# A decay product two units ahead, scatters in one unit, and layer 2 ordered by kind

## The chip, the cores and the metric

The kernel runs on one core of a Trainium2 chip. The core has five engines that run their own instruction streams and wait for each other by semaphores: TensorE (PE in the profile; its weight loads are listed as PEld), VectorE (DVE), ScalarE (ACT), GpSimd (POOL) and SyncE (SP), which mostly issues transfers. The metric is the device time of one execution in microseconds, as the median of several runs.

## The reference

The program computes three things in a row. First a decaying linear attention over 4 batches, 8 heads, 768 positions and a head size of 64: in blocks, `out = (q k^T * D) v + (q * lam^(i+1)) S`, with a state `S = lam^block * S + (k * lam^(block-1-i))^T v`. The result is 3072 rows of 512 numbers. Then a first mixture of experts over these rows:

```python
logits = x @ w_gate + modality_bias[modality_id]
e_idx = np.argmax(logits, axis=1)
gate_w = softmax(logits)[row, e_idx]
for e in range(8):
    mask = e_idx == e
    h = np.maximum(x[mask] @ w1[e], 0.0)          # 512 -> 1024
    out[mask] = gate_w[mask, None] * (h @ w2[e])  # 1024 -> 512
```

Then a second mixture of the same shape with other weights, without a bias, for those rows only for which `x @ w_skip > 0`; its result is added to the row, and the other rows pass through.

## The kernel before

**Precision.** Large products are made from two float32r parts of each operand, a high and a low one: high times high, low times high and high times low. A raw weight `raw1` or `raw2` is split by ScalarE into the high part (`w1h`, `w2h`, a rounding copy) and by VectorE into the low part (`w1l`, `w2l`, the raw value less the high one). A float32 product of the attention runs as two passes, each with its own weight load.

**Attention.** The work is cut into N = 24 units `(c, b)`: six chunks of 128 positions times four batches, chunk by chunk. Instructions stand in an order written out by hand in the loop over `i` (`tc.manual_schedule()`), and each engine runs its own in that order. For a unit, `stage_s` makes the scores and VectorE multiplies them by the decay mask `dm` into `P`; `stage_t` transposes k and VectorE scales it into `kd`; `stage_q` (GpSimd) makes `qs`, q times the decay table `ltab`, and `t0`, the old state times the block decay; `stage_inter` multiplies `qs` by the state; `stage_av` multiplies `P` by v and ScalarE copies the sum to `xts`; `stage_kv` makes the state's update, which VectorE adds to `t0` into `sc_` and ScalarE copies into `sd`; `stage_x` transposes the output to rows and SyncE stores them in `xs1`. Units of the first chunk have no state and no `qs`, those of the last chunk no `t0`. k and q are loaded four units ahead. Before the first unit `spin` keeps TensorE at work with products of a constant, and the table `ltab` is built by VectorE from a tile `lead`.

**Routing.** After each chunk the four units' logits are made (`route_1`, `route_2`), the expert is chosen (`route_3`, a chain of small VectorE instructions that ends in the one-hot `oh` and the running counts `rs`), ranks and gates follow (`route_4`), and `route_5` scatters an index row for each of four row groups from GpSimd's queue into the table `tab[0]`. The list `sc` holds the scatters that are still to come. In unit 17 the counts so far choose the expert with the most rows; its weights and its first 256 rows are fetched while the attention still runs (`load_ix`, `gather_x`, `ld_w1_half`, `ld_w2`). `behind` makes a weight load wait for the gathered rows.

**The layers.** Each mixture works through slots of 256 rows of one expert, as two blocks j of 128. `trans_x` transposes the gathered rows into `xth` and `xtl`; `layer1` makes 8 column groups f of 128 with 12 products each, and after every second f ScalarE (`hh`) and VectorE (`hl`) take the result from one of three banks; `layer2` makes for a block 8 chunks c with 3 products each, and ends with a scaled result `x2r`. `steps[f]` are functions that run after group f and its evacuation, `mids[f]` those between its products and its evacuation, `hooks[n]` those after chunk n. `first1` and `first2` write out the first slot of each layer, in which the last routing step, the slot table (`table`, a chain of VectorE instructions in three parts, each started by `next(tb)`), the index reads, the gathers and the weight splits of what follows all have to be done. Later slots run in `slots`.

Of the kernel before, what the change touches and what calls it, by code (L numbers as in the profile page):

```python
# [9 lines left out]
F32 = mybir.dt.float32  # L10
# [8 lines left out]
P = 128  # L19
# [16 lines left out]
def body(ctx: ExitStack, tc: tile.TileContext, qkv, cpk, w1, w2, wgr, out, dbg=None):  # L36
# [284 lines left out]
    def low_w2(c, eng=nc.vector):  # L321
        eng.tensor_tensor(out=w2l[c], in0=raw2[:, 2 * c:2 * c + 2], in1=f32(w2h[c]), op=ALU.subtract)  # L322
# [97 lines left out]
    with ExitStack() as actx:  # L420
# [45 lines left out]
        def spin(n):  # L466
            for _ in range(n):
                nc.tensor.matmul(banks[6][:, 0:P], keepm, keepm, start=True, stop=True)

        lead = wk.tile([P, NP, P], F32, tag="qs", name="lead")  # L470
# [72 lines left out]
        def stage_q(i):  # L543
            c, b = units[i]
            if c == 0:
                return
            qs = wk.tile([P, NP, P], F32, tag="qs", name="qs")
            nc.gpsimd.tensor_tensor(out=qs, in0=loaded[i][1], in1=ltab, op=ALU.mult)
            qss[i] = qs
            if c < NC - 1:  # L550
                t0 = wk.tile([P, NP, C], F32, tag="t0", name="t0", bufs=1)
                nc.gpsimd.tensor_tensor(out=t0, in0=sc_[b], in1=bc(ltab[:, :, P - 1:P], [P, NP, C]), op=ALU.mult)
                t0s[i] = t0
# [42 lines left out]
        spin(8)  # L596
        stage_s(0)
        stage_t(0)
        spin(2)
        for i in range(N):  # L600
            rc = i // B - 1 if i >= B and i % B == 0 else None
            rd = i // B - 1 if i >= B and i % B == 1 else None
            if i + 1 < N and i + 1 not in qss:
                stage_q(i + 1)
# [32 lines left out]
            if i == N - 3:  # L637
                stage_q(N - 1)
                got0 = gather_x(0, 0, 4 * B * P)
# [9 lines left out]
            for _ in range(2 if i in (17, 18, 21, 22) else 1):  # L649
                if sc:  # L650
                    route_5(*sc.pop(0))
# [156 lines left out]
    def layer2(which, kk, j, hooks={}, cs=range(8)):  # L808
# [10 lines left out]
        if 7 not in cs:  # L819
            return  # L820
# [20 lines left out]
    def first1():  # L841
        tb = table(0)

        def last_x():
            high(1, (2, 3))
            low(1, (2, 3))
            stage_x(NC * B - 1, ptr[0])
            route_1()
            high_w2(0)
            low_w2(0, nc.gpsimd)  # L850

        def mid():
            route_2(NC - 1)
            route_3(NC - 1)

# [27 lines left out]
    def first2():  # L883
# [3 lines left out]
        layer1(0, {0: la, 3: lambda: rb(pcnt[1]), 4: lambda: next(tb), 5: lambda: split_w2([1]),  # L887
               6: lambda: split_w2([2]), 7: lambda: split_w2([3])}, mids={1: rk}, lead=True)
# [11 lines left out]
        layer2(1, 0, 0)  # L900
        next(tb)
        fl = flag(1, 1)
        layer2(1, 0, 1, {5: lambda: trans_x(1, 1, ptr), 6: lambda: split_next(1, 1, fl)})

# [178 lines left out]
```

## Time and profile before

| | before |
|---|---|
| median of 3 runs | 682.98 us (682.23 to 684.29) |
| the profiled execution's own time | 682.28 us |
| its span, first to last instruction | 680.4 us |
| TensorE busy | 659.4 us (97%), 5408 products |
| weight loads busy | 588.4 us (86%) |
| VectorE busy | 435.5 us (64%) |
| ScalarE busy | 261.5 us (38%) |
| GpSimd busy | 225.0 us (33%) |
| mean granted TensorE clock | 0.994 |

The profile is of one execution, and all times in it count from its first instruction. The time of that execution is 1.9 us longer than its span. A busy TensorE is not one at its peak: products are pipelined, and their ends are modelled. L764 and the like are lines of the kernel before. A row's bracket gives the idle time before it and what ended it.

### The profile page before, as it was taken

What the parts mean: (1) busy time and instruction counts of PE and PEld (TensorE: products, weight loads), DVE (VectorE), ACT (ScalarE), POOL (GpSimd) and SP (SyncE); (2) the same over time, 40 slices, a digit from 0 to 9 for tenths busy, and PEclk for the clock granted to TensorE, in tenths of its full rate; (3) what the DMA queues carried; (4) which work ended last, traced back from release to release, by engine and by line L of the source; (5) the groups of instructions that cost most, each with busy time, mean ns of one, the idle gap of its engine ahead of it and who ended that gap; (6) DMA issues with size and microseconds to landing.
All of it is one profiled execution on the core that took longest, in us unless ns stands there. A gap on an engine that the chain in (4) does not pass through costs nothing. (4 is left out here: it accounts for less than half of the span.)

```text
span 680.4 us, 16335 instructions
## 1 busy us (share of the span) xinstructions
PE 659.4 (97%) x5408; PEld 588.4 (86%) x5408; DVE 435.5 (64%) x1147; ACT 261.5 (38%) x461; POOL 225.0 (33%) x284
## 2 busy tenths in 40 slices
PE   9999999999999999999999999998999999999993
PEld 8899987888988898889889988897999899988892
DVE  7655678764887716869778227967236575759650
ACT  5444435422212225822122227441224644566520
POOL 4265656443242231243422333323211112203321
PEclk9999999999999999999999999999999999999997
DMA  8978777459331133893211211724616557657500
GB/s 261 301 217 217 227 206 247 156 172 373 126 118 52 50 127 119 289 302 131 86 50 31 94 66 37 257 92 116 240 63 241 180 176 276 218 188 263 190 4 30
DMA packets 60797, 112.08 MB, mean 165 GB/s; under 512 B 18816, under 2 KB 18944, under 8 KB 60528
## 3 DMA queue, kind: packets, MB, share of 16 engines
q1 hardware_dynamic: 48688, 89.07, 39.6%
q0 software_dynamic: 9744, 20.47, 9.0%
q8 instruction: 63, 1.03, 0.7%
q10 hardware_dynamic: 2224, 0.86, 0.5%
q14 instruction: 78, 0.64, 0.3%
HBM read 86.44 MB, written 30.06 MB: 171 GB/s over the span
## 5 line engine op out<-in xcount | busy, mean ns | idle before, releaser
L764 PE MATMUL bank<-xth,w1h 128*128 128x256 f32 x672 | 188.3, 281 | 1.1 <-DVE hl L774 0.8
L764 PE MATMUL bank<-xtl,w1h 128*128 128x256 f32 x672 | 185.8, 278 | 1.7 <-issue 1.6
L764 PE MATMUL bank<-xth,w1l 128*128 128x256 f32 x672 | 186.7, 278 | 0.0
L814 PE MATMUL bank<-w2h,hh 128*128 128x512 f32 x360 | 144.7, 402 | 0.0
L815 PE MATMUL bank<-w2l,hh 128*128 128x512 f32 x360 | 140.9, 392 | 1.1 <-DVE w2l L322 1.1
L816 PE MATMUL bank<-w2h,hl 128*128 128x512 f32 x360 | 141.3, 393 | 0.3 <-DVE hl L796 0.3
L764 PEld LDWEIGHTS bank<-xth,w1h 128*128 128x128 f32 x672 | 126.4, 188 | 3.5 <-issue 1.1
L764 PEld LDWEIGHTS bank<-xth,w1l 128*128 128x128 f32 x672 | 126.6, 188 | 2.1 <-DVE hl L774 1.7
L764 PEld LDWEIGHTS bank<-xtl,w1h 128*128 128x128 f32 x672 | 126.0, 188 | 1.4 <-DVEq L836 0.7
L771 ACT ACTIVATE hh<-bank 128x512 fp32r<-128x512 f32 x84 | 50.3, 598 | 182.7 <-PE bank L764 172.1
L161 POOL DMA_INDIRECT out_dram<-x2r,it x43 | 52.5, 1220 | 192.6 <-DVE x2r L829 105.6
L774 DVE SCALAR_TENSOR_TENSOR hl<-bank,hh 128x512 fp32r<-128x512 f32 (+1 forms) x100 | 58.4, 601 | 84.7 <-ACT hh L771 84.3
L717 DVE CUSTOM_DVE_ANT_0 xtl<-x2r,wgb 128x512 fp32r<-128x512 f32 x108 | 74.3, 692 | 14.4 <-issue 9.1
L816 PEld LDWEIGHTS bank<-w2h,hl 128*128 128x128 f32 x360 | 67.6, 188 | 16.0 <-DVE hl L796 0.7
L815 PEld LDWEIGHTS bank<-w2l,hh 128*128 128x128 f32 x360 | 67.7, 188 | 15.7 <-DVE w2l L322 2.5
L161 POOL DMA_INDIRECT tab<-pk,rows x28 | 33.3, 1190 | 141.0 <-issue 85.8
L814 PEld LDWEIGHTS bank<-w2h,hh 128*128 128x128 f32 x360 | 67.7, 188 | 12.8
L165 POOL DMA_INDIRECT xg<-xs,it x54 | 58.2, 1078 | 26.4 <-issue 13.7
L322 DVE TENSOR_TENSOR w2l<-raw,w2h 128x1024 fp32r<-128x1024 f32 x47 | 54.7, 1219 | 4.7 <-ACT w2h L319 2.8
L826 ACT ACTIVATE x2r<-bank,it 128x512 f32<-128x512 f32 x26 | 17.9, 689 | 100.3 <-PE bank L816 89.4
L319 ACT CAST w2h<-raw 128x1024 fp32r<-128x1024 f32 x48 | 49.1, 1051 | 18.8 <-issue 12.0
L316 DVE TENSOR_TENSOR w1l<-raw,w1h 128x512 fp32r<-128x512 f32 x88 | 53.9, 685 | 0.5 <-ACT w1h L315 0.3
(211 smaller groups left out, 835.5 us busy)
## 6 DMA issues: line engine op xcount, KB each, us to landing
raw<-in_w_dram SPq DMA_DIRECT2D x96, 512.0 KB, 6.3
kq<-in_qkv_dram SPq DMA_DIRECT2D x48, 256.0 KB, 4.2
xs<-x2r SPq DMA_DIRECT2D x28, 256.0 KB, 2.1
v<-in_qkv_dram SPq DMA_DIRECT2D x24, 256.0 KB, 3.9
xs<-xr SPq DMA_DIRECT2D x24, 256.0 KB, 6.2
xs<-xgm SPq DMA_DIRECT2D x7, 512.0 KB, 4.8
wgb<-in_wgr_dram SPq DMA_DIRECT2D x1, 2304.0 KB, 13.6
xg<-xs,it POOLq DMA_INDIRECT x54, 4.1
```

What stands on the lines that cost most here:

```text
L161: nc.gpsimd.indirect_dma_start(out=dst, out_offset=bass.IndirectOffsetOnAxis(ap=idx, axis=0), in_=rows, in_offset=None, bounds_check=dst.s ...
L165: return nc.gpsimd.indirect_dma_start(out=rows, out_offset=None, in_=src, in_offset=bass.IndirectOffsetOnAxis(ap=idx, axis=0), bounds_chec ...
L316: nc.vector.tensor_tensor(out=w1l[c][:, s], in0=raw1[:, c, s], in1=f32(w1h[c][:, s]), op=ALU.subtract)
L319: nc.scalar.copy(out=w2h[c], in_=raw2[:, 2 * c:2 * c + 2])
L322: eng.tensor_tensor(out=w2l[c], in0=raw2[:, 2 * c:2 * c + 2], in1=f32(w2h[c]), op=ALU.subtract)
L717: nc.vector.tensor_tensor_reduce(out=xtl[kk % 2][:, :, j * P:(j + 1) * P], in0=x2r[kk % 2][j].rearrange("p (c t) -> p c t", t=P), in1=wgb[ ...
L764: nc.tensor.matmul(o, w[c][:, fs], x[:, c, :], start=(n == 0), stop=(n == 11))
L771: nc.scalar.activation(out=a, in_=pt, func=AF.Relu)
L774: nc.vector.scalar_tensor_tensor(out=b[:, q_], in0=pt[:, q_], scalar=0.0, in1=f32(a[:, q_]), op0=ALU.max, op1=ALU.subtract)
L814: nc.tensor.matmul(p2[j], a, w2h[g][:, i], start=(n == 0), stop=False)
L815: nc.tensor.matmul(p2[j], a, w2l[g][:, i], start=False, stop=False)
L816: nc.tensor.matmul(p2[j], b, w2h[g][:, i], start=False, stop=(n == 7))
```

## The change

- `spin` makes products of 64 columns instead of 128, 15 and 1 of them instead of 8 and 2.
- `stage_q` makes only `qs` and runs two units ahead instead of one, with three buffers instead of two (the tile `lead` has one of them); `t0` moves into a new function `stage_d`, one unit ahead as before, with two buffers instead of one. The separate call of `stage_q` for the last unit goes.
- In unit 17 four scatters are issued, in unit 18 none; before it was two and two.
- The first low part `w2l` of the first layer is made by VectorE after `route_3`, and not by GpSimd.
- In `first2` ranks and gates (`rb`) come ahead of the evacuation of group 3; the high parts of w2 stay in the steps 5 to 7, the low ones come after layer 1; the table's third part comes before layer 2; and layer 2 runs over both blocks by kind, first all products of `hh` with `w2h`, then of `hl` with `w2h`, then of `hh` with `w2l`. The transposes for slot 1 stand after 39 of the 48 products, before after 42.
- The end of `layer2` becomes a function `finish`.

```diff
@@ -318,8 +318,8 @@
     def high_w2(c):
         nc.scalar.copy(out=w2h[c], in_=raw2[:, 2 * c:2 * c + 2])
 
-    def low_w2(c, eng=nc.vector):
-        eng.tensor_tensor(out=w2l[c], in0=raw2[:, 2 * c:2 * c + 2], in1=f32(w2h[c]), op=ALU.subtract)
+    def low_w2(c):
+        nc.vector.tensor_tensor(out=w2l[c], in0=raw2[:, 2 * c:2 * c + 2], in1=f32(w2h[c]), op=ALU.subtract)
 
     def split_w2(cs=range(4)):
         for c in cs:
@@ -465,9 +465,9 @@
 
         def spin(n):
             for _ in range(n):
-                nc.tensor.matmul(banks[6][:, 0:P], keepm, keepm, start=True, stop=True)
-
-        lead = wk.tile([P, NP, P], F32, tag="qs", name="lead")
+                nc.tensor.matmul(banks[6][:, 0:C], keepm, keepm[:, 0:C], start=True, stop=True)
+
+        lead = wk.tile([P, NP, P], F32, tag="qs", name="lead", bufs=3)
         nc.vector.memset(lead, 0.0)
 
         def ladder(r, lm, first, acts=False):
@@ -544,11 +544,14 @@
             c, b = units[i]
             if c == 0:
                 return
-            qs = wk.tile([P, NP, P], F32, tag="qs", name="qs")
+            qs = wk.tile([P, NP, P], F32, tag="qs", name="qs", bufs=3)
             nc.gpsimd.tensor_tensor(out=qs, in0=loaded[i][1], in1=ltab, op=ALU.mult)
             qss[i] = qs
-            if c < NC - 1:
-                t0 = wk.tile([P, NP, C], F32, tag="t0", name="t0", bufs=1)
+
+        def stage_d(i):
+            c, b = units[i]
+            if 0 < c < NC - 1:
+                t0 = wk.tile([P, NP, C], F32, tag="t0", name="t0")
                 nc.gpsimd.tensor_tensor(out=t0, in0=sc_[b], in1=bc(ltab[:, :, P - 1:P], [P, NP, C]), op=ALU.mult)
                 t0s[i] = t0
 
@@ -593,15 +596,17 @@
             return [nc.sync.dma_start(out=raw1[:, c:c + 2, n * D:n * D + D], in_=src[:, c:c + 2, n * D:n * D + D]) for c in (0, 2)][0]
 
         sc = []
-        spin(8)
+        spin(15)
         stage_s(0)
         stage_t(0)
-        spin(2)
+        spin(1)
         for i in range(N):
             rc = i // B - 1 if i >= B and i % B == 0 else None
             rd = i // B - 1 if i >= B and i % B == 1 else None
-            if i + 1 < N and i + 1 not in qss:
-                stage_q(i + 1)
+            if i + 2 < N:
+                stage_q(i + 2)
+            if i + 1 < N:
+                stage_d(i + 1)
             if rc is not None:
                 route_1()
             if i == 20:
@@ -635,7 +640,6 @@
             if 0 < i < N - 1:
                 stage_s(i + 1)
             if i == N - 3:
-                stage_q(N - 1)
                 got0 = gather_x(0, 0, 4 * B * P)
             if i < N - 1:
                 stage_x(i, psX)
@@ -646,7 +650,7 @@
                 sc += [(rd, t) for t in range(B)]
             if i + 1 < N:
                 stage_t(i + 1)
-            for _ in range(2 if i in (17, 18, 21, 22) else 1):
+            for _ in range(4 if i == 17 else 2 if i in (21, 22) else 1):
                 if sc:
                     route_5(*sc.pop(0))
             if 2 <= i < 4:
@@ -816,8 +820,25 @@
             nc.tensor.matmul(p2[j], b, w2h[g][:, i], start=False, stop=(n == 7))
             if n in hooks:
                 hooks[n]()
-        if 7 not in cs:
-            return
+        if 7 in cs:
+            finish(which, kk, j)
+
+    def layer2_wide(which, hooks):
+        n = 0
+        for kind in range(3):
+            for j in range(2):
+                js = slice(j * P, (j + 1) * P)
+                for c in range(8):
+                    x = (hh, hl, hh)[kind][c // 4][:, c % 4, js]
+                    w = (w2h, w2h, w2l)[kind][c // 2][:, c % 2]
+                    nc.tensor.matmul(p2[j], x, w, start=(kind == 0 and c == 0), stop=(kind == 2 and c == 7))
+                    if n in hooks:
+                        hooks[n]()
+                    n += 1
+                if kind == 2:
+                    finish(which, 0, j)
+
+    def finish(which, kk, j):
         g = XG(which, kk)[j]
         ix = IT(which, kk)[:, j]
         gate = ix[:, 1:2].bitcast(F32)
@@ -847,11 +868,11 @@
             stage_x(NC * B - 1, ptr[0])
             route_1()
             high_w2(0)
-            low_w2(0, nc.gpsimd)
 
         def mid():
             route_2(NC - 1)
             route_3(NC - 1)
+            low_w2(0)
 
         def late():
             route_4(NC - 1)
@@ -884,8 +905,10 @@
         la, rk, rb = router(itl)[1:4]
 
         tb = table(1)
-        layer1(0, {0: la, 3: lambda: rb(pcnt[1]), 4: lambda: next(tb), 5: lambda: split_w2([1]),
-               6: lambda: split_w2([2]), 7: lambda: split_w2([3])}, mids={1: rk}, lead=True)
+        layer1(0, {0: la, 4: lambda: next(tb), 5: lambda: high_w2(1), 6: lambda: high_w2(2), 7: lambda: high_w2(3)},
+               mids={1: rk, 3: lambda: rb(pcnt[1])}, lead=True)
+        for c in range(1, 4):
+            low_w2(c)
         for i in range(1, 4):
             load_ix(1, i)
         got = gather_x(1, 1)
@@ -897,11 +920,9 @@
                               reason="the rows first")
         ld_w2(e)
         gather_x(1, 2)
-        layer2(1, 0, 0)
         next(tb)
         fl = flag(1, 1)
-        layer2(1, 0, 1, {5: lambda: trans_x(1, 1, ptr), 6: lambda: split_next(1, 1, fl)})
-
+        layer2_wide(1, {38: lambda: trans_x(1, 1, ptr), 41: lambda: split_next(1, 1, fl)})
         return fl, is_full(ei[1][0:1, 3 * KT + 1:3 * KT + 2])
 
     def slots(which):
```

## Rows read from the trace of the kernel before

**Rows 1.** TensorE's waits over the whole run: us in total, times, longest.
```profile
PE bank L366 <- DMA xg<-xs,it: 2.1, 3, 1.0
...
PE pmi L137 <- DVE oh L125: 0.8, 1, 0.8
```
**Rows 2.** Two stretches by engine: busy us (instructions), granted clock, DMA.
```profile
0.00:8.00 8.00, 6.74 (x40) 6.19 (x40) 4.59 (x9) 5.04 (x11) 5.48 (x43) 1.00 0.75 237
465.00:469.00 4.00, 4.00 (x19) 3.28 (x18) 3.72 (x17) 0.00 (x0) 1.91 (x3) 1.00 0.33 80
```
**Rows 3.** Timeline of the start: start, us, engine, line, instructions.
```profile
1.26 3.49 PEld L468 LDWEIGHTS bank<-keepm 128*128 128x128 f32 x16 [1.26 <-DVE keepm L464]
...
4.97 2.08 PE L522 MATMUL bank<-kq 64*128 64x128 f32 x16
...
7.08 1.42 DVE L529 TENSOR_TENSOR P<-bank,dm 128x256 f32<-128x256 f32 x4
...
7.37 0.53 PEld L468 LDWEIGHTS bank<-keepm 128*128 128x128 f32 x4
```
**Rows 4.** Timeline of units 17 to 19.
```profile
95.81 0.98 POOL L161 DMA_INDIRECT tab<-pk,row  x1 [0.30 <-issue]
96.27 1.85 DVE L206 TENSOR_TENSOR eid<-t_p,t_g 128x8 f32<-128x8 f32 x1
...
96.81 1.28 POOL L548 TENSOR_TENSOR qs<-kq,ltab 128x512 f32<-128x512 f32 x1
...
97.13 0.60 PE L537 MATMUL bank<-ident,kq 128*128 128x128 f32 x4
...
98.14 1.16 PE L561 MATMUL bank<-qs,sd 128*128 128x128 f32 x8 [0.42 <-POOL qs L548]
...
100.04 0.98 PE L569 MATMUL bank<-P,v 128*64 128x128 f32 x13 [0.16 <-DVE P L529]
```
**Rows 5.** Timeline from the last early scatter to the gathered rows.
```profile
100.96 0.97 POOL L161 DMA_INDIRECT tab<-pk,row  x1 [0.30 <-issue]
...
106.96 0.40 SPq L351 DMA_DIRECT2D it<-tab  x1
...
110.78 1.07 POOL L165 DMA_INDIRECT xg<-xs,it  x1 [0.15 <-issue]
...
115.77 1.06 PE L561 MATMUL bank<-qs,sd 128*128 128x128 f32 x8
...
119.23 1.09 PE L569 MATMUL bank<-P,v 128*64 128x128 f32 x16
```
**Rows 6.** Transfers issued from 95 to 120 us: median us to landing.
```profile
xg<-xs,it POOLq DMA_INDIRECT x2, 6.6
```
**Rows 7.** Timelines at units 16 and 23: one instruction, alone and beside GpSimd's.
```profile
89.97 0.19 DVE L122 SCALAR_TENSOR_TENSOR sc<-d,pri 128x32 f32<-128x32 f32 x1
...
125.74 2.39 POOL L322 TENSOR_TENSOR w2l<-raw,w2h 128x1024 fp32r<-128x1024 f32 x1 [4.21 <-ACT w2h L319]
125.75 2.43 DVE L122 SCALAR_TENSOR_TENSOR sc<-d,pri 128x32 f32<-128x32 f32 x1
```
**Rows 8.** Timelines of the second layer's first slot, four engines.
```profile
453.70 0.69 DVE L774 SCALAR_TENSOR_TENSOR hl<-bank,hh 128x512 fp32r<-128x512 f32 x1 [1.35 <-ACT hh L771]
...
459.19 1.04 ACT L319 CAST w2h<-raw 128x1024 fp32r<-128x1024 f32 x1
...
460.07 2.35 DVE L322 TENSOR_TENSOR w2l<-raw,w2h 128x1024 fp32r<-128x1024 f32 x2
...
461.33 0.50 PE L815 MATMUL bank<-w2l,hh 128*128 128x512 f32 x1 [1.07 <-DVE w2l L322]
...
463.66 1.41 POOL L165 DMA_INDIRECT xg<-xs,it  x1 [4.93 <-DMA it<-tab]
466.86 1.08 POOL L165 DMA_INDIRECT xg<-xs,it  x1 [1.79 <-issue]
...
471.17 0.66 PE L366 MATMUL bank<-ident,xg 128*128 128x128 f32 x4 [0.98 <-DMA xg<-xs,it]
```

## The prediction

> **What bounds the kernel now.** I read the list of TensorE's waits first, then the stretches around each wait as a timeline of all engines, and last the landing times of the transfers. TensorE sets the end: of a 680.4 us span it is busy for 659.4, and the products follow each other. A change can therefore only win back the few places where TensorE stands still. The list of waits has the larger of them [rows 1]: 2.1 us for gathered rows (three times, two of them in the attention's last unit, one in layer 2 of the second layer) and 0.8 for the routing's `oh`. The timelines add 1.07 for a low part of w2 [rows 8], one late `qs` [rows 4], and the time before the first unit, in which products run at half pace [rows 3]. The change touches each of these places. All costs below are shifts of TensorE's next product.
>
> **The spin at the start.** Sixteen loads, one for each of the two passes of eight products, occupy 3.49 us, 0.218 apart [rows 3]. In a later stretch four such loads take 0.53, about 0.11 apart [rows 3]. So the first stretch runs at 1.2 GHz and the later one at 2.4, though the view of stages gives a granted clock of 1.00 for all of 0 to 8 us [rows 2] and the pace alone tells. The step is near 7.0 us, where the products of the first unit change pace; before it TensorE had run since 1.26. The edit makes 15 products of 64 columns out of 8 of 128, which is 30 loads instead of 16, each still of 128 columns by 128 rows. No row shows such a load under so short a product. Bounds: if a pass costs its columns, it halves to 0.109 and the spin takes 3.3 us. If the load sets the pace, it stays at 0.218. I take the load, because the loads fill their stretch without a gap: nothing shows that one takes less than its 0.218. Then 26 of the 30 passes fit between 1.26 and 7.0, four more at 0.11 end at 7.45, and the scores of unit 0 begin near 7.5 instead of 4.97. They then run at full pace, about 1.1 us where they took 2.08, and VectorE can take them up 1.2 us after their start, at 8.7 instead of 7.08 [rows 3]: **+1.6 us**. From there on TensorE and VectorE hand over to each other without a gap, so the delay stays. At the lower bound the scores begin 0.2 us sooner, but VectorE takes up `P` at 7.08 without idle time before it [rows 3], so it is busy until then: 0. Cutting the second spin from 4 passes of 128 to 2 of 64 columns gives nothing: TensorE waits there for the mask product `P`.
>
> The rule of the Trainium skill on this stands in its page "TensorE: Matmul & The Clock Gate", section "LDWEIGHTS (loading the stationary operand)": the time of a load goes with the stationary operand's columns, and the product's own length does not enter. Its figure for 128 columns, 107 ns, agrees with the 0.11 of the later stretch; by it as an estimate 30 loads at half pace would take 6.4 us, against 3.3 if columns counted.
>
> **`qs` two units ahead, four scatters in one unit.** In unit 17 GpSimd does two scatters and only then `qs` for unit 19 (96.81 to 98.09). VectorE's `eid`, eight columns wide, lasts 1.85 us, from 96.27 to 98.12, until that `qs` product has run [rows 4]; an instruction four times as wide takes 0.19 [rows 7]. TensorE's transposes end at 97.57 (four from 97.13, 0.109 each), and its next batch starts at 98.14. The products on `P`, whose mask VectorE could make only after `eid`, go on at 100.04 [rows 4]. After the edit `qs` for 19 is finished a unit earlier, and only scatters stand in GpSimd's queue then. `eid` falls to 0.19, `P` is done 1.66 us sooner, by 98.4, and the products on it can go on at 97.57 + 1.0 (eight products) + 0.1 = 98.7: **-1.3 us**. What is queued behind the four scatters: at a pitch of 0.98 + 0.30 (the one at 95.81 [rows 4]) they leave at 94.5, 95.8, 97.1 and 98.4 and end at 99.4; then come `qs` for 20, 1.28 like its neighbour, to 100.7, and the decay product for unit 19 to 101.4. The batch that needs that `qs` comes a whole unit, about 5 us, after the one of 98.14. VectorE wants the decay product near 100.4 and gets it 1 us late; the state it feeds is used four units on, and the next `P`, which waits behind it on VectorE, is wanted only after TensorE's transposes and its batch on `qs`, some 2 us. Without that cover it would cost up to 1.0. In the other units no wait for `qs` is there to be won.
>
> **The first gather.** Index rows for slot 0 are read by SyncE only when the fourth scatter of this group has landed: it leaves at 100.96, the read at 106.96, the gather at 110.78, and its rows take 6.6 us [rows 5, 6]. TensorE ends its batch of 115.77 at 116.66, does eight transposes (0.87) and starts the next at 119.23 [rows 5]: 1.6 us lost, of which 1.5 is wait. With the last scatter leaving 2.5 us sooner the read leaves near 104.4 and the gather near 107.2 (GpSimd's last `qs` is done by 105.5, since it no longer waits for a buffer). The rows land by 113.8 and 115, before TensorE asks for them at 115.3 and 115.8: **-1.5 us**. Bounds: 0 if the scatters land as late as now, since the first half of w1 is on the queues then; 1.6 if all is hidden. The w2 load, which SyncE holds back behind this gather, starts about 3 us sooner, which no wait asks for.
>
> **First w2l on VectorE.** GpSimd's subtraction lasts 2.39 us from 125.74. VectorE's `sc`, 32 columns, starts at 125.75 and lasts 2.43, where the same instruction takes 0.19 a few units earlier [rows 7]. `oh` follows it, and TensorE's counting product waits for that [rows 1]. Without the subtraction on GpSimd `sc` is 2.24 us sooner, and the wait goes. But VectorE now does the subtraction itself, at 1.2 us (two take 2.35 [rows 8]), so all that stands behind it on VectorE (the high-low split, row numbers, the scatters, the slot table, the other low parts) comes only 2.24 - 1.2 = 1.0 us sooner. TensorE runs into the low parts in layer 2, where the last ones are just in time today. I take **-1.1 us**; bounds -0.5 and -1.5.
>
> The Trainium skill has the cause: "SBUF — State Buffer", section "SBUF: two separate sides", says that a VectorE instruction with two SBUF inputs and a GpSimd instruction that reads SBUF contend for one port pair, which is an exclusive lock for a whole instruction. The 2.43 beside the 2.39 agrees with it.
>
> **The second layer's first slot.** TensorE waits 1.07 us for the second low part of w2, until 461.33, and 0.98 for gathered rows of slot 1, until 471.17 [rows 8]. A product of this layer takes 0.23 (4.00 us hold 18 loads, one of them cut by the edge [rows 2]). Layer 2 starts at 461.33 - 1.07 - 8 x 0.23 = 458.5 or so. Ordered by kind, the low parts are needed after 32 products, at 466, and VectorE has them near 463.8, since nothing but the order of its work changes: that wait goes. A new one comes in: the high part of the fourth chunk (459.19 + 1.04 [rows 8]) is wanted after six products, at 459.9: 0.4 us. The transposes now stand after 39 products instead of 42, so TensorE reaches them at 458.5 + 0.4 + 39 x 0.23 = 467.9, and nine products remain behind them instead of six. What is late next is the gather. Routing moved ahead of VectorE's split uses idle time that stands there today (1.35 us before 453.70 [rows 8]); the slot table, which follows it, and so index read and gather, come 0.5 us sooner. The gather's second half left 3.2 us after the first (463.66 and 466.86 [rows 8]); the scatters above follow each other at 1.3, and no row names what held it. If this stays, the rows land at 470.7, and four transposes and nine products (0.44 + 2.1) lead to 473.2; today 471.17 + 0.44 + 6 x 0.23 gives 473.0: 0. If it goes, the rows land 1.8 us sooner, near 468.9, layer 1 of the next slot can start near 471.4, and the wait of ScalarE's and VectorE's split for the flag leaves 1.5. Bounds 0 and -1.7. I take **-1.5**, since nothing in the code makes one half wait for more than the other.
>
> **Sum:** +1.6 - 1.3 - 1.5 - 1.1 - 1.5 = -3.8 us. The profiled execution took 682.28, so 678.5. The median of the runs, 682.98, is 0.7 above it, so 679.2 on its scale. A difference of 0.3%, 2.05 us, is about what a measurement of this kernel can tell from none.
>
> **Rivals.**
> The second half of the gather stays 3.2 us behind: -2.3, so 680.7. For it: its cause isn't seen. Against: the scatters of the attention follow each other at 1.3.
> The spin costs its columns alone: -5.4, so 677.6. Against it is the fullness of the loads' stretch.
> The first gather is as late as now: -2.3, so 680.7; the landing of 6.6 us speaks for it, the 2.5 us head start against.
> The change does nothing on balance, because each freed wait is met by the next one (high part, low parts, gather): near 682.5.
> On the other side: the clock. With half the columns per load TensorE streams less before 7.0, and the step to 2.4 GHz may come later. Each us of delay costs half a us of TensorE's work. Slower by 2.05 needs 5.85 us of cost, a step 11.7 us later, at 18.7. At 20 us it would be 685.7. Against it: the loads keep TensorE as occupied as before.
>
> **Numbers.** Forecast 0.38 (its own range 678.2 to 680.2), late second half 0.22, free spin 0.13, late first gather 0.10, nothing on balance 0.10, late clock 0.07. The range leaves out the late clock and the lowest tail of the free spin: 676.8 to 682.5. Faster by over 0.3%, below 680.9: 0.36 + 0.12 + 0.13 + 0.05 + 0.02 = 0.68. Within: 0.26. Slower: 0.06.
>
> **What would show it.** Thirty spin loads ending near 7.4 and the first `P` near 8.7; `eid` and `sc` at 0.2 us; no wait at the first gather's transposes; no wait for `oh`; a wait of 0.4 for `w2h`; two gather halves 1.4 apart and a wait for them under 0.6. The prediction fails if the clock steps up later than 8 us, or if the two gathers land no sooner.

## The result and the profile after

The changed kernel is slower: 687.68 us, the median of nine runs (684.05 to 689.55), against 682.98 of the kernel before in nine runs beside it (682.23 to 684.74). The ratio is 1.0064 [1.0046, 1.0083]. Two more comparisons of the same kernel gave 1.0054 [1.0037, 1.0070] and 1.0053 [1.0030, 1.0076]. The profiled execution took 686.78 us with a span of 684.9, so its span is 4.5 us longer than before.

I compared the two traces by marks, the start of the same TensorE work in both. The last two columns are shifts, summed up to the mark. "Products on `qs`" are the batch in which a unit multiplies `qs` by the state.

| mark | before | after | shift | predicted |
|---|---|---|---|---|
| unit 4, products on `qs` | 24.78 | 28.52 | +3.7 | +1.6 |
| unit 19, the same | 98.14 | 101.30 | +3.2 | +0.3 |
| unit 20, the same | 104.21 | 110.87 | +6.7 | +0.3 |
| first product of layer 1 | 120.26 | 126.27 | +6.0 | -1.2 |
| layer 1, behind the wait for `oh` | 129.49 | 133.82 | +4.3 | -2.3 |
| first slot after it, transposes | 145.38 | 150.09 | +4.7 | |
| first layer, later slot | 231.47 | 234.28 | +2.8 | |
| second layer, layer 2 of its first slot | 458.50 | 461.82 | +3.3 | -2.3 |
| second layer, layer 1 of its second slot | 473.06 | 477.53 | +4.5 | -3.8 |

Two places lose: the start (+3.7) and units 18 to 20 (+2.9 net, as unit 19 first wins 0.6). At the wait for `oh`, where the `w2l` part acts, 1.7 are won, and 1.9 near 225 us, where nothing was changed. Of the list of TensorE's waits, that of the kernel after shows:
```profile
PE bank L366 <- DMA xg<-xs,it: 2.9, 2, 2.2
PE bank L572 <- DVE P L529: 2.0, 2, 1.8
```
The wait for `oh` [rows 1] is gone. The one for gathered rows has grown, now all in the second layer, and one of 1.8 us for the masked scores `P` is new.

**The start.** Timeline of the kernel after:
```profile
1.25 6.47 PEld L468 LDWEIGHTS bank<-keepm 128*128 128x128 f32 x30 [1.25 <-DVE keepm L464]
...
7.85 2.08 PE L522 MATMUL bank<-kq 64*128 64x128 f32 x16
...
9.96 1.42 DVE L529 TENSOR_TENSOR P<-bank,dm 128x256 f32<-128x256 f32 x4 [2.86 <-PE bank L522]
...
12.87 1.16 PE L522 MATMUL bank<-kq 64*128 64x128 f32 x16
```
The thirty loads take 0.216 each from first to last, as sixteen did [rows 3]. But unit 0's scores still take 2.08 us at 7.85, and only unit 1's, at 12.87, take 1.16: TensorE reaches 2.4 GHz between the two, not near 7.0. The trace's records of the granted clock, which begin with the first full one, begin at 12.54; those of the kernel before at 7.03.

**Units 18 and 19.** Timeline of the kernel after, then its stages (busy us of PE, PEld, DVE, ACT, POOL, then granted clock, DMA share and GB/s):
```profile
98.67 0.69 PE L585 MATMUL bank<-v,kd 128*64 128x64 f32 x16
...
99.28 1.16 PE L522 MATMUL bank<-kq 64*128 64x128 f32 x16
...
99.56 0.98 POOL L161 DMA_INDIRECT tab<-pk,row  x1 [0.30 <-issue]
...
100.01 0.17 DVE L206 TENSOR_TENSOR eid<-t_p,t_g 128x8 f32<-128x8 f32 x1
...
100.84 0.98 POOL L161 DMA_INDIRECT tab<-pk,row  x1 [0.30 <-issue]
...
102.12 0.98 POOL L161 DMA_INDIRECT tab<-pk,row  x1 [0.30 <-issue]
...
102.54 0.33 SPq L438 DMA_DIRECT2D v<-in_qkv_dram  x1
102.62 0.42 DVE L590 TENSOR_TENSOR sc<-t,bank 128x256 f32<-128x256 f32 x1 [2.08 <-PE bank L537]
...
104.10 1.29 DVE L529 TENSOR_TENSOR P<-bank,dm 128x512 f32<-128x512 f32 x2 [1.05 <-PE bank L564]
...
104.84 1.93 PE L572 MATMUL bank<-P,v 128*64 128x128 f32 x12 [1.84 <-DVE P L529]
```
```profile
102.00:104.00 2.00, 0.96 (x7) 0.68 (x6) 0.42 (x1) 0.81 (x2) 1.86 (x2) 1.00 0.23 36
104.00:106.00 2.00, 1.16 (x8) 0.85 (x10) 1.89 (x3) 0.59 (x1) 2.00 (x3) 0.67 0.89 47
106.00:108.00 2.00, 2.00 (x28) 2.00 (x24) 0.00 (x0) 0.55 (x1) 1.41 (x2) 0.50 0.93 261
```
`eid` lasts 0.17, as predicted. Then comes what I had not looked for. The last product of unit 18 on `kd` ends at 99.36. SyncE's next load of v, which needs that product alone for its buffer, leaves at 102.54, 3.2 us later, and VectorE's `sc`, which needs the same products, starts at 102.62 (its other operand, `t0`, stands ahead of the scatters in GpSimd's queue). Both start as the last of the four scatters is on GpSimd. What they wait for is TensorE's semaphore, and the trace has its updates: the one for that product comes at 102.53. Five more, for products that ended between 100.44 and 103.00, come together at 104.07 to 104.33. The scores for VectorE's next `P` are among them: they are done at 100.44, and `P` starts at 104.10, 1.05 us after `sc` has ended. TensorE then stands for 1.84 us, and the granted clock falls to 0.50 for 3.4 us (104.70 to 108.11 in its records).

**The last unit and layer 1.** Timelines of the kernel after:
```profile
123.05 1.04 PE L366 MATMUL bank<-ident,xg 128*128 128x128 f32 x8
123.34 1.25 POOL L161 DMA_INDIRECT tab<-pk,row  x1 [0.30 <-issue]
...
124.89 1.32 ACT L369 CAST xth<-bank 128x512 fp32r<-128x512 f32 x2 [1.66 <-PE bank L366]
...
131.77 0.19 DVE L122 SCALAR_TENSOR_TENSOR sc<-d,pri 128x32 f32<-128x32 f32 x1
```
The transposes no longer wait for rows, but TensorE comes 6 us later. ScalarE's `xth` starts 0.8 us after the last of them, beside a scatter of the last unit. VectorE's `sc` of the routing takes 0.19, where it took 2.43 [rows 7].

**The second layer's first slot.** Timeline of the kernel after:
```profile
458.94 0.16 DVE L152 TENSOR_TENSOR rows<-rr,nm 128x2 uint32<-128x2 f32 x1 [2.16 <-DMA tab<-pk,rows]
...
468.30 1.48 POOL L165 DMA_INDIRECT xg<-xs,it  x1 [5.39 <-DMA it<-tab]
...
471.50 1.15 POOL L165 DMA_INDIRECT xg<-xs,it  x1 [1.72 <-issue]
...
472.11 0.66 PE L366 MATMUL bank<-ident,xg 128*128 128x128 f32 x4 [0.67 <-DMA xg<-xs,it]
...
474.96 0.66 PE L366 MATMUL bank<-ident,xg 128*128 128x128 f32 x4 [2.19 <-DMA xg<-xs,it]
```
The halves of the gather are 3.2 us apart, as before [rows 8]. The wait for `w2l` is gone, and TensorE waits 2.86 us for rows instead.

### The profile page after: what moved, and what is told of

Read it like the earlier page. It is cut to its first block, busy times and chain, and to the rows that moved or that the text cites. A ratio compares the mean times of both kernels' runs of the same rounds, so it can differ in the third digit from the quotient of the medians.

```text
span 684.9 us, 16356 instructions
## 1 busy us (share of the span) xinstructions
PE 664.2 (97%) x5420; PEld 593.7 (87%) x5420; DVE 432.0 (63%) x1148; ACT 262.2 (38%) x461; POOL 223.0 (33%) x283
## 5 line engine op out<-in xcount | busy, mean ns | idle before, releaser
L818 PE MATMUL bank<-w2h,hh 128*128 128x512 f32 x344 | 138.1, 402 | 0.0
L820 PE MATMUL bank<-w2h,hl 128*128 128x512 f32 x344 | 135.2, 393 | 0.3 <-DVE hl L800 0.3
L819 PE MATMUL bank<-w2l,hh 128*128 128x512 f32 x344 | 134.4, 391 | 0.3 <-DVE w2l L322 0.2
L820 PEld LDWEIGHTS bank<-w2h,hl 128*128 128x128 f32 x344 | 64.6, 188 | 15.3 <-DVE hl L800 0.7
L819 PEld LDWEIGHTS bank<-w2l,hh 128*128 128x128 f32 x344 | 64.7, 188 | 14.0 <-DVE w2l L322 1.2
L818 PEld LDWEIGHTS bank<-w2h,hh 128*128 128x128 f32 x344 | 64.7, 188 | 12.2
```

The lines of the kernel that those rows point to most:

```text
L818: nc.tensor.matmul(p2[j], a, w2h[g][:, i], start=(n == 0), stop=False)
L819: nc.tensor.matmul(p2[j], a, w2l[g][:, i], start=False, stop=False)
L820: nc.tensor.matmul(p2[j], b, w2h[g][:, i], start=False, stop=(n == 7))
```

## The experiments

The theory after these traces: 64 columns put off the clock's step; the row of four scatters holds up the engines that wait for TensorE. The rivals: the spin is late by its loads alone; the new order of layer 2 costs the time; the stop is an accident of one execution.

The runs fall into five sets, each on one chip with its own runs of the kernel before: 1 to 4 (683.86), 5 to 8 (683.79), 9 to 12 (684.28), 13 to 16 (682.05), 17 and 18 (683.85). In the table "late" is the time from the end of unit 18's last `kd` product to SyncE's v load, "unit 4" the start of its `qs` products, and "full" the time at which the trace's records of the granted clock begin, with full speed. A bracketed 15 marks the spin of 15 and 1 products of 128 columns; without it 128 means 8 and 2, and 64 means 15 and 1.

| kernel | columns, scatters in unit 17 | median us | ratio [95%] | late | unit 4 | full |
|---|---|---|---|---|---|---|
| before | 128, 2 | 682.98 | | 0.04 | 24.78 | 7.0 |
| after | 64, 4 | 687.68 | 1.0064 | 3.19 | 28.52 | 12.5 |
| 1 | 128, 4 | 684.83 | 1.0020 [1.0004, 1.0036] | 3.14 | 24.78 | 7.0 |
| 2 | 64, 2 | 683.77 | 0.9996 [0.9985, 1.0008] | 1.74 | 27.98 | 11.5 |
| 3 | 128, 2 | 682.25 | 0.9970 [0.9958, 0.9981] | 1.74 | 24.78 | 4.7 |
| 4 | 128, 4 | 684.86 | 1.0018 [1.0006, 1.0029] | 3.16 | 24.81 | 4.5 |
| 5 | 64, 4 | 687.62 | 1.0054 [1.0037, 1.0070] | 3.26 | 28.53 | 12.6 |
| 6 | 64, 2 | 684.98 | 1.0018 [1.0003, 1.0032] | 1.78 | 27.66 | 10.5 |
| 7 | 128, 2 | 682.88 | 0.9985 [0.9974, 0.9996] | 1.80 | 24.73 | 6.1 |
| 8 | 128, 2 | 683.70 | 0.9998 [0.9988, 1.0009] | 1.80 | 24.82 | 5.6 |
| 9 | 128, 2 | 682.01 | 0.9968 [0.9955, 0.9982] | 1.78 | 24.84 | 6.3 |
| 10 | 128, 2 | 682.72 | 0.9970 [0.9955, 0.9985] | 1.81 | 24.85 | 5.2 |
| 11 | 128 (15), 2 | 682.43 | 0.9978 [0.9963, 0.9992] | 1.81 | 25.08 | 4.2 |
| 12 | 128, 0 | 650.04 | 0.9508 [0.9485, 0.9531] | 0.04 | 24.61 | 5.0 |
| 13 | 128 (15), 2 | 680.75 | 0.9982 [0.9965, 0.9999] | 0.04 | 26.04 | 6.2 |
| 14 | 128 (15), 4 | 679.94 | 0.9967 [0.9951, 0.9984] | 0.04 | 25.43 | 4.9 |
| 15 | 64, 2 | 682.14 | 1.0003 [0.9993, 1.0013] | 0.04 | 28.43 | 12.4 |
| 16 | 128, 3 | 678.85 | 0.9965 [0.9948, 0.9982] | 0.04 | 24.65 | 4.2 |
| 17 | 64, 4 | 687.75 | 1.0053 [1.0030, 1.0076] | 3.17 | 29.07 | 13.8 |
| 18 | 128 (15), 2 | 681.49 | 0.9967 [0.9948, 0.9987] | 1.77 | 25.22 | 4.5 |

**1, the changed kernel with the old spin.**
```diff
-        spin(15)
+        spin(8)
...
-        spin(1)
+        spin(2)
...
-                nc.tensor.matmul(banks[6][:, 0:C], keepm, keepm[:, 0:C], start=True, stop=True)
+                nc.tensor.matmul(banks[6][:, 0:P], keepm, keepm, start=True, stop=True)
```


> The changed kernel with the spin of before (8 and 2 products of 128 columns). Theory: halving the spin's columns only moved the clock's step from 7.0 to 12.5 us and so put every later unit 3.7 us back, and the stop of TensorE in front of unit 20 (3.5 us) is another matter. Then the step is back at 7.0, the products on qs of unit 4 start near 24.8 instead of 28.5, the stop near 101 us stays, and the time is 687.7 - 3.7 = 684.0, with a spread like that of the changed kernel. Rival: the stop in front of unit 20 hangs on the late start, and goes with it: 680.5.

The start is back at 24.78, but the kernel is still slower than before, so the spin isn't the only cause. Timeline of this kernel at unit 18:
```profile
94.94 0.69 PE L585 MATMUL bank<-v,kd 128*64 128x64 f32 x16
...
98.77 0.33 SPq L438 DMA_DIRECT2D v<-in_qkv_dram  x1
```
The 3.1 us are there without the new spin.

**2, the kernel before with the new spin alone** (the diff of 1 from right to left).

> The kernel before with nothing but the new spin (15 and 1 products of 64 columns). Theory (late clock): step near 12.5 us, unit 4 near 28.5, and 683.0 + 3.7 = 686.7. Rival (the prediction's own term: the loads set the pace, the clock steps at 7.0 as it did): 684.6. A second rival: VectorE or the transfers take up the delay within the attention, 683.0 to 684.0.

The first units are 3.2 us late, yet the end is the same: this alone is no slower kernel, and the second rival held.

**3, the changed kernel with old spin and old scatters.**
```diff
-            for _ in range(4 if i == 17 else 2 if i in (21, 22) else 1):
+            for _ in range(2 if i in (17, 18, 21, 22) else 1):
```


> The changed kernel with the spin of before and with two scatters in each of units 17 and 18 as before; qs two units ahead stays. Theory: the stop in front of unit 20 and the half clock from 104.7 to 108.1 us come from the four scatters in one unit. Then both are gone: 684.0 - 3.5 + 1.5 (the first gather late again) = 682.0. Rival: the stop comes from the order of qs and the decay product on GpSimd, or from nothing in the code: the stop stays and the time is 684 or above.

Faster than before, and 2.6 us less than 1 by the medians on the same chip (0.50% by the ratios): that is the price of four scatters in a row. With two, the late start is 1.74.

**4, as 1, with the old first slot of the second layer** (`layer2` block by block, `rb` in step 3, `split_w2` in steps 5 to 7).
```diff
-        layer2_wide(1, {38: lambda: trans_x(1, 1, ptr), 41: lambda: split_next(1, 1, fl)})
+        layer2(1, 0, 1, {5: lambda: trans_x(1, 1, ptr), 6: lambda: split_next(1, 1, fl)})
```


> The changed kernel with the spin of before and with the second layer's first slot as before (layer 2 block by block, routing and low parts in the old places). Theory: that part costs 1.2 us in the changed kernel (3.3 us behind the kernel before at its start, 4.5 at its end), because VectorE's row numbers, now ahead of a split, wait 2.2 us for GpSimd to leave the loop before: 684.0 - 1.2 = 682.8. Rival: the scatters at the end of the loop only landed late in that one execution, and the part gains its 0.7 to 1.5 us otherwise: 684.7 to 685.5.

No different from 1: in this company the new order of layer 2 neither costs nor wins. The rival that it costs the time is out.

**5, the changed kernel again; 6, it with the old scatters** (the diff of 3).

> The changed kernel once more, beside the runs of before that the next three share, because the spin's cost inside the changed kernel (687.68 against 684.83 without the new spin, 2.9 us) was read from two chips. Theory: the late clock's 3.7 us at unit 4 stay in the end in part: 2 to 3 us above the same kernel with the old spin, that is some 4 us above before. Rival: the spin costs nothing in the end, as it cost nothing alone, and the changed kernel is 1 us above before.

> The changed kernel, new spin included, with two scatters in each of units 17 and 18 as before. Theory (the four scatters in one unit are the loss, the late start is met by later waits): as with the old spin, 1.6 us below before, at most 1 us more than that. Rival (the late start is the loss): 2 us above before.

The stop repeats, so it is no accident, and the four scatters again cost 2.6 us (687.62 to 684.98; 0.36% by the ratios). The theory failed here: the late start costs too. With 1, 3 and 5 this makes a square: ratios 0.9970 with 128 columns and two scatters, 1.0018 with 64 and two, 1.0020 with 128 and four, 1.0054 with both. Either spoils the gain of the rest, and the two nearly add up. The corners with 128 columns have the spin of 8 and 2 products.

**7, the kernel before with the first `w2l` on VectorE alone.**
```diff
-            low_w2(0, nc.gpsimd)
...
             route_3(NC - 1)
+            low_w2(0)
```


> The kernel before with nothing but the first low part of w2 on VectorE. Theory (the prediction's term): the first sc of the last routing falls from 2.4 to 0.2 us, the wait for oh goes, 1.1 us faster than before. Rival: what TensorE gains there it loses at the next wait (row numbers, low parts of w2, gather): no change.

0.9 us faster: this part does what it says.

**8, as 3, with the old second slot too** (what is left is `qs` and `w2l`; diffs of 1, 3 and 4).

> The changed kernel with the spin of before, two scatters in each of units 17 and 18, and the second layer's first slot as before; left of the change are qs two units ahead and the first w2l on VectorE. Theory: the second layer's first slot is worth nothing, so the gain of the run that kept it stays whole: 1.6 us faster than before. Rival: with the four scatters gone the new order of layer 2 does pay, as the prediction had it, and its 1.5 us are missing here: as before.

As slow as before, so the rival held. `eid` remains at 1.85 when the scatters stay two and two, so `qs` two units ahead wins nothing; whether it loses what `w2l` wins isn't shown, as 3 and 9, which differ by it, have the same ratio. Against 3 the new second slot is worth 1.9 us by the ratios, and 9 against 7 makes it 1.2.

**9, `w2l` and the second slot; 10, the same with twelve tiny products of constants before the last unit's transposes.**
```diff
             if i == N - 1:
+                pad(12)
                 trans_x(0, 0, [psT, psK])
```


> The kernel before with the first low part of w2 on VectorE and the new first slot of the second layer; the old spin, the old qs order and the old scatters. Theory (the parts add): the first is worth 0.9 alone, the second 1.9 where the four scatters were undone (0.9970 against 0.9998 of before), so 2.8 us faster than before, 0.4%. Rival: the second slot pays only with qs two units ahead, which changes when its transfers run: 0.9 us faster.

> The run before this one with twelve single-pass products of 8 columns, results unused, put on TensorE in the wait for the first gathered rows: as many instructions as the new spin adds. All six profiles with the old spin have a stop of 1.5 to 1.8 us at 225 to 228 us that waits for nothing the profile shows, all four with the new spin have none. Theory: the stop hangs on where the instructions lie, and goes with the added ones: another 1.6 us faster. Rival: it hangs on the time at which the loop is reached, or is chance: as the run before, or up to 0.6 us slower for the added products.

9 is 2.2 us faster than before. 10 asked what was won near 225 us. Timeline of 9 there:
```profile
226.49 0.28 PE L764 MATMUL bank<-xtl,w1h 128*128 128x256 f32 x1 [1.64 <-issue]
```
A stop of 1.4 to 1.6 us without a releaser stands between 222 and 229 us in all nine profiles whose TensorE program has the old length before it (before, 1, 3, 4, 7 to 9, 12, 16), and in none of the eleven with 24 more TensorE instructions ahead of it. In the nine a 16 KB transfer of q8, a DMA queue that the profile calls "instruction", begins 0.7 to 1.0 us before the stop and ends 1.4 to 1.7 before TensorE goes on, which points to the fetching of TensorE's instructions but doesn't show it, as such transfers pass without a stop in the others. 10 has those 24 as its pad, and the stop is gone. Its end is no sooner: it waits 2.42 us for the second layer's rows instead, and then has half the clock for 3.4 us (469.4 to 472.8).

**11, the kernel before with fifteen and one products of 128 columns.**
```diff
-        spin(8)
+        spin(15)
...
-        spin(2)
+        spin(1)
```


> The kernel before with a spin of 15 products of 128 columns and 1 more behind the mask product, the number of the new spin with the columns of the old one. Theory (it is the halved columns that put the clock's step off): the step comes at 4.5 to 7.0 us as with the old spin, the loads run at 0.11 from there, unit 4 starts 0.5 to 1.6 us later than before. Rival (a spin of 30 loads delays the scores, and the step waits for the work behind it): step at 10 to 12.5, unit 4 near 28, as with 64 columns.

This parts loads from columns. Timeline of its start:
```profile
1.26 4.80 PEld L468 LDWEIGHTS bank<-keepm 128*128 128x128 f32 x30 [1.26 <-DVE keepm L464]
...
6.18 1.16 PE L522 MATMUL bank<-kq 64*128 64x128 f32 x16
```
The same thirty loads take 4.80 us instead of 6.47, because the clock's step falls among them, and unit 0's scores run at full pace. Unit 4 is 0.3 us late, against 3.2 in 2: so 2.9 come from the columns. That it ends sooner than the kernel before may go with the stop near 225 us, which it doesn't have; in 10 the stop's going alone won nothing.

**12, as 1, with the four scatters of unit 17 left out** (the rows of that chunk are then missing from the routing table, and the second layer has fewer slots; only the attention's part can be compared).
```diff
-                sc += [(rd, t) for t in range(B)]
+                if rd != 3:
+                    sc += [(rd, t) for t in range(B)]
```


> The changed kernel with the old spin and without the four table scatters of unit 17: left out, so the tokens of that group aren't found by the first layer's gathers. Theory (the scatters in a row hold up TensorE's completion signals): the signal of the last product of unit 18 on kd comes within 0.1 us of its end instead of 3.2 later, VectorE's sc of unit 18 and P of unit 19 follow at once, and TensorE's 2.0 us wait and the half clock behind it are gone: 2.5 to 4 us faster than with them (684.8). Rival (TensorE's signals are late there for another reason, such as its instructions being fetched): still late by 1.7 to 3.2 us, and 684 or above.

Timeline of 12 at unit 18:
```profile
96.24 0.69 PE L585 MATMUL bank<-v,kd 128*64 128x64 f32 x16 [1.35 <-DVE kd L539]
...
96.97 0.33 SPq L438 DMA_DIRECT2D v<-in_qkv_dram  x1
...
98.00 0.41 DVE L590 TENSOR_TENSOR sc<-t,bank 128x256 f32<-128x256 f32 x1
```
The load leaves 0.04 us after the product. Unit 20's products start at 104.05, in 1 at 107.36: without the scatters the 3.3 us are gone.

**13, `w2l`, second slot and the spin of 11; 14, the changed kernel with 128 columns; 15, as 13 with 64; 16, as 1 with three scatters in unit 17.**
```diff
-            for _ in range(4 if i == 17 else 2 if i in (21, 22) else 1):
+            for _ in range(3 if i == 17 else 2 if i in (21, 22) else 1):
```


> The kernel before with the spin of 15 and 1 products of 128 columns, the first w2l on VectorE and the new first slot of the second layer; qs and scatters as before. Theory (the parts add): 1.5 (that spin alone) + 2.3 (the other two together) = 3.8 us faster than before. Rival (what is won before the second layer's first slot is waited for at its gathered rows): 2.3 us, as without the spin.

> The changed kernel with its spin's columns restored to 128 and nothing else, 15 and 1 products as it has. Theory (the halved columns cost the late clock step, 2.9 us at unit 4 between the two spins of 15): step at 4 to 7 us, unit 4 near 25.1, and about 2.5 us less than the changed kernel's 687.6, so 685.1. Rival (the late start is mostly met by later waits, as it was where the spin alone was changed): 686.5 or more.

> The first kernel of this set with the changed kernel's spin, 64 columns, in place of 128. Theory: unit 4 near 28 again and 1.3 to 2.9 us slower than the first of this set. Rival: 0, as the new spin cost nothing beside the old one where it was changed alone.

> The changed kernel with the old spin and three scatters in unit 17, the fourth in unit 18. With two there TensorE's signal for the last product of unit 18 on kd comes 1.75 us late and nothing waits for it long; with four 3.2 us late; with none at once. Theory (the signals are held until the row of scatters is nearly through): 1.8 to 3 us late, TensorE's wait at P between 1.3 and 2.0 us, time between 682.2 (two) and 684.8 (four). Rival: as with four.

13 was to add its parts up to 3.8 us and is 1.3 faster. 14, expected at 685.1, is faster than before. 15 against 13 is the columns again: unit 4 is 2.4 us later, the end 1.4. 16 was to give the dose, two, three or four scatters, and couldn't: in this set nothing was late, whatever stood on GpSimd. So this set can't price the scatters. Timeline of 14:
```profile
95.58 0.69 PE L585 MATMUL bank<-v,kd 128*64 128x64 f32 x16
...
96.31 0.33 SPq L438 DMA_DIRECT2D v<-in_qkv_dram  x1
...
97.35 0.42 DVE L590 TENSOR_TENSOR sc<-t,bank 128x256 f32<-128x256 f32 x1
...
99.03 0.98 POOL L161 DMA_INDIRECT tab<-pk,row  x1 [0.30 <-issue]
...
107.13 0.40 SPq L351 DMA_DIRECT2D it<-tab  x1
...
110.27 1.07 POOL L165 DMA_INDIRECT xg<-xs,it  x1 [0.81 <-DMA it<-tab]
```
Here the same four scatters run and the load leaves after 0.04; every update of TensorE's semaphore at units 18 and 19 comes within 0.05 us of its product's end. Units 18 to 20 take 9.74 us where before took 11.23: this is the 1.3 of the prediction. And the last scatter leaves 1.9 us sooner than before, but the index read doesn't (107.13; 106.96 before [rows 5]).

**17, the changed kernel a third time; 18, it with 128 columns and the old scatters.**

> The changed kernel as it is, once more. In all profiles from three chips TensorE's signal for the last product of unit 18 on kd comes 1.7 us late with two scatters in unit 17 and 3.2 late with four; on a fourth chip it comes at once with two, three and four. Theory (the chip, or the state it is in, decides, and the four scatters cost only where signals are held): where the signal comes at once, the changed kernel is 1.4 to 2.5 us above the same kernel with full columns (0.9967 of before), so between 0.3 us below and 0.3 us above before; where it is held, 3.7 us or more above before, as twice measured. Rival: 3.7 us above before, whatever the signal does.

> The changed kernel with its spin's columns restored to 128 and with two scatters in each of units 17 and 18. Theory: the clock steps early, no row of four scatters stands in front of unit 20, and it is 2 to 3 us faster than before whether signals are held or not. Rival: where signals are held, the last unit's four scatters take it back, and it is within 1 us of before.

18 is 2.4 us faster than before, 17 3.9 slower: on one chip, the two lines of code make up 6.3 us. 18 has two scatters with signals late by 1.77, so the theory held and the rival didn't.

The time from unit 4's products on `qs` to those of unit 20 leaves the start out and puts all twenty profiles on one scale. Signals here are the updates of TensorE's semaphore. With `qs` in its old place and two and two scatters it is 79.4 us, whether signals are late (2, 7, 9 to 11) or not (before, 13, 15). With `qs` two units ahead it is 78.0 where nothing is late (14, 16); where signals are late, 79.8 with two and two scatters (3, 6, 8, 18) and 81.1 to 82.6 with four (after, 1, 4, 5, 17). 12, without scatters, has 79.4, with a wait of 1.35 us for `kd`.

## Why the prediction was wrong

**The spin (+1.6; measured +3.7).** "If the load sets the pace, it stays at 0.218" was right. The Trainium skill too has the time of a load go with the columns of what is loaded ("TensorE: Matmul & The Clock Gate", section "LDWEIGHTS (loading the stationary operand)"), and the same 0.216 under 64-column products agrees. The step that failed is "The step is near 7.0 us": I carried it over from the kernel before. It comes between 4.2 and 7.0 in all fourteen profiles with 128 columns and between 10.5 and 13.8 in all six with 64. A step later than 8 us was one of the two signs of failure that the prediction named. The rival that I gave 0.07, a late clock, had the mechanism, and its rate of half a us for each us of delay was a little high: between 11 and 2 the clock comes 7.3 us later and unit 4 2.9, between 13 and 15 6.2 and 2.4, so 0.4 each. Against it I had put that the loads keep TensorE as occupied as before; they did, and the step still came late. At the end of the kernel the columns cost 1.2 us (2 against 11, across two sets) and 1.4 (15 against 13) with few other parts, but 2.3 to 3.5 by the ratios with `qs` ahead (after or 5 against 1, 6 against 3 or 18; only 6 and 18 differ by the columns alone). Why so little of 2.9 us is left in the one company and all of it in the other stays open.

**`qs` and four scatters (-1.3; measured +2.9).** The term itself was right where nothing was late: `eid` is 0.17, and 14 wins 1.5. What failed is the step "what is queued behind the four scatters". I followed GpSimd's own queue and priced it at up to 1.0 us. The cost came on other engines: SyncE and VectorE start up to 3.3 us late on TensorE's products, as its semaphore is updated that late, and TensorE then stands 1.84 us. The half clock behind that adds 1.5: in 4's profile, which has the same stop without it, units 4 to 20 take 81.1 us, in 1's 82.6. Leaving the scatters out takes the delay away (12), two in place of four halve it (3, 6). So the number of scatters sets the delay on those chips. What holds the updates back isn't shown; no record names it. A row of scatters isn't enough for it, as 13 to 16 show, and the profile of before, whose chip isn't on record, shows no delay either. What differs there is open, and so is the effect of three. It reaches beyond this place: the five traces without the delay record 621 to 624 updates of that semaphore in the whole run, the fourteen with it, and 12 on the chip of 9 to 11, 563 to 589.

**The first gather (-1.5; measured 0).** Its lower bound holds: "0 if the scatters land as late as now". What failed is that the read would leave as much sooner as the last scatter: in 14 this scatter leaves 1.9 us sooner, but what it writes lands at 106.92 (106.76 before), so the index read leaves 0.2 later and the gather 0.5 sooner than before. In 1 the read did leave 1.8 sooner, at 105.17, and the gather only 0.3. The 0.10 for this rival was too small.

**The first `w2l` (-1.1; measured -1.7 in the marks, -0.9 in 7 alone).** Right in mechanism and within its bounds by 7; the wait is gone, and `sc` takes 0.19. In 2 and 11, which keep the subtraction on GpSimd, `sc` takes 0.19 too, and the delay falls on its neighbours (`rs`, 2.82 us for four, and `d`, 1.60), so `sc` alone doesn't tell.

**The second layer's first slot (-1.5; measured +1.2).** The ordering by kind did remove the wait for `w2l`, with a wait of 0.2 for `w2h` for the predicted 0.4. The step that failed is "I take -1.5, since nothing in the code makes one half wait for more than the other": the halves stay 3.2 us apart in every profile but 12 (2.1), the rival of 0.22. What holds the second half isn't shown. Another 2.16 us are lost ahead of it by `rows`: the record puts the wait down to a transfer of the table, but GpSimd has an instruction of its sequencer, `INC_SWDGE_SEM`, at the end of the loop before (456.51 to 458.91), and the trace has VectorE wait ahead of `rows` for two semaphores that are updated at 458.80 and 458.82, as it ends. The wait is 0.8 to 2.2 in seven of the twenty profiles, each time until 0.12 us or so after such updates, and 0.04 in the others. As a whole this part was worth 1.9 us in one comparison (3 against 8, two sets), 1.2 in another (9 against 7, two sets) and nothing in the third (4 against 1).

**Not predicted.** The stop near 225 us went by itself, 1.9 us won at that mark.

Without the late clock, and without the four scatters or on the chip where they cost nothing, the rest wins 2.1 to 2.4 us by the ratios (3, 9, 14, 16, 18 at 0.9965 to 0.9970; 9 is without `qs` ahead), against the predicted 5.4 for the four terms behind the spin; these five beat both kernels.

## What to carry to other kernels

A warm-up of TensorE is worth the clock step that it brings about, so when its products change, look at when the products behind it change pace, and take nothing over from the old trace. When instructions of one queue are gathered into a row, look at who else starts late while the row runs, on every engine, and not only at what is queued behind it. A stall of TensorE near 2 us was here followed in a third of the cases by 3.4 us at half the clock, and then costs more than itself.

## What the runs showed of the hardware

- SyncE's load started 1.74 to 1.81 us after the TensorE product that it waits for with two indirect transfers in a row on GpSimd, 3.14 to 3.26 with four, 0.04 with none; and 0.04 with two, three or four in one set of runs, and with two in the profile of before. TensorE's semaphore was updated some 0.02 us before the load each time.
- Halving the columns of the warm-up's products, with the loads back to back in both, moved the step to full clock from 4.2 to 7.0 us to 10.5 to 13.8.
- TensorE stopped 32 times for 1.5 us or more between 10 and 600 us in the twenty profiles. Eleven of these stops, of 1.61 to 2.42 us (after, 1, 3, 5, 10, 11, 12, 14, 17 twice, 18), had a granted clock of 0.50 for 3.4 us behind them or from their last 0.4 us on; 21, of 1.50 to 2.20, hadn't.
- A stop of 1.4 to 1.6 us that waits for nothing came and went with 24 instructions more, 100 us and more before it, and TensorE went on 1.4 to 1.7 us after the end of a 16 KB transfer of the queue q8, called "instruction". It looks like the place of the code; no record says so.
